# Second slot of a group: the output products first, the value products a slot later, and two PSUM banks that change roles

## The chip, the cores and the metric

One NeuronCore of a Trainium2 chip runs the whole program. The metric is the device time of one execution in microseconds (us), lower is better; a kernel's time is the median of its runs.

## The reference

Attention over pooled keys, then a feed-forward block whose activation is SoLU with a layer norm. Cut to what is computed:

```python
kv_pool = kv.reshape(B, H//4, 4, W//4, 4, C).mean(axis=(2, 4))
k = v = kv_pool.reshape(B, -1, C) @ w_sr          # 768 keys of 128
s = scale * (q @ k.T); a = exp(s - max(s)); a /= a.sum() + 1e-9
x = a @ v                                          # B*N = 49152 tokens of 128
h = x @ w_in                                       # 128 -> 1024
u = h * softmax(h)
ln = (u - mean(u)) / sqrt(var(u) + 1e-6) * g_ln
out = ln @ w_out                                   # 1024 -> 128
```

There are B = 4 batches of N = 12288 tokens. All inputs are float32; the kernel keeps float32-like accuracy by splitting operands in a high and a low 16-bit part and summing three products.

## The kernel before

A tile is 128 tokens, there are 384, and four tiles make a group (96 groups, 24 to a batch). The main loop (lines 892 to 969) runs one slot per tile and is a software pipeline written out by hand: the order of the calls in a slot is the order of the instructions on every engine and on SP's DMA queue, since the program is scheduled by hand. In a slot, work on tiles of very different age stands side by side:

- `scores_pe(slot + 1)`: six products of TensorE (PE) give the scores **s** (L386) of the next tile. `scores_exp`: VectorE (DVE) takes their maximum **nm** (L402), ScalarE (ACT) their exponential (L403) and the high half of the probabilities **phl** (L407). `scores_split`: DVE makes the low half (L415). `scores_turn`: SP turns phl into **pT** by a DMA transpose (L422); below, such a transfer is a *p*.
- `values`: PE multiplies the pT of a whole group with the values in 18 products of 512 columns into one bank **xa** (L453). They are spread over four slots. `values_out` (ACT, **xh**) and `values_split` (DVE, **xl**, L464) read xa out in halves.
- `hidden_pe(slot - 9)`: six products give **h** (L505). DVE takes a minimum **junkd** (L513), ACT an exponential **e** (L529), DVE the product **u** (L543), GpSimd (POOL) the halves **uhl** (L560, L566). `hidden_turn`: SP turns uhl into **uT** by a DMA transpose (L580), below a *u*.
- `final_pe(slot - 13)`: 24 products of 128 columns give a quarter of the bank **o** (L631). `final_half` (L674) scales it to **ob**, two quarters at a time, and `final_store` sends ob out.
- `values_norm` (POOL, **zz**, L479), `values_recip` (DVE, **rz**, L487) and `values_recip_u` (ACT, L492) make a group's scale factors.
- The keys of the next batch are loaded (L216), added on POOL (**ka**, L227), multiplied on PE (**pk**, L235), copied by ACT (L238) and later turned on PE (**pv**, L286) and copied again (L291). `PLAN` (lines 860 to 868) says in which slots of a batch.

Text below names a slot by its number modulo 4: R0, R1, R2, R3. PE's order before is s, xa x4, h, o in R1; xa x1, s, xa x4, h, o in R2 and R3; xa x1, s, xa x3, h, o in R0. In R1 the products of a new group begin in xa and in o.

PSUM has eight banks. Six belong to a ring `ps_r` of three double banks in which s and h take turns: s(slot + 1) takes what h(slot - 11) held and waits for DVE's u; h(slot - 9) takes what s(slot) held and waits for DVE's phl. One bank, `ps_x`, holds xa, and the keys' pk and pv while xa is not in use; the other, `ps_o`, holds o.

SP issues every DMA of the main loop in program order. In R3 it is p, p, u, and then the load of queries **qf**; in R0 u; in R1 p, u and the store; in R2 p, u; and a load of **kv** in many groups.

Of the kernel before, what the change touches and what calls it, by code (L numbers as in the profile page):

```python
# [11 lines left out]
F32 = mybir.dt.float32  # L12
# [6 lines left out]
ALU = mybir.AluOpType  # L19
AX = mybir.AxisListType  # L20

P = 128
# [7 lines left out]
TPB = NTOK // P  # L30
WARM = 14
NT = B * TPB
GT = 4
GPB = TPB // GT
NG = NT // GT
# [9 lines left out]
LAV = 2  # L45
XSP = 5
NORM = 6
LH = 10
LO = 13
FSC = 12  # L50
# [4 lines left out]
ROOM = {NT - 9: 0, NT - 8: 0, NT - 7: 0, NT - 3: 1, NT - 2: 1, NT - 1: 1}  # L55

TAIL = """
U:-1 xa:-1 xh:-1 h:1 o:-4 M:0 xl:-1 J:-1 h:2 hi:-1 E:0 lo:-1 M:1 zz:-1 E:1 o:-3 U:0 h:3
J:0 U:1 zz:0 hi:0 rc:-1 h:4 M:2 ob:-3 rc:0 hi:1 f2:-2 lo:0 rz:-1 E:2 turn:-1 xa:0 turn:0
J:1 lo:1 M:3 st:-3 U:2 o:-2 E:3 J:2 M:4 U:3 E:4 U:4 h:5 xh:0 turn:1 hi:2 f:-2 lo:2 xl:0  # L60
hi:3 J:3 turn:2 M:5 h:6 hi:4 h:7 M:6 E:5 rz:0 lo:3 E:6 o:-1 U:5 M:7 turn:3 o:0 J:4 U:6
f2:-1 o:1 h:8 h:9 o:2 lo:4 E:7 turn:4 U:7 o:3 hi:5 M:8 hi:6 J:5 M:9 ob:-2 lo:5 hi:7 lo:6
# [15 lines left out]
def kernel(  # L78
# [15 lines left out]
    nc = tc.nc  # L94

    dmt = ctx.enter_context(tc.tile_pool(name="dmt", bufs=2))
# [8 lines left out]
    ps_x = ctx.enter_context(tc.tile_pool(name="ps_x", bufs=1, space=bass.MemoryType.PSUM))  # L105
# [34 lines left out]


    state = {}

    def kv_alloc(b):
        for n, w, dt, bufs in (
# [81 lines left out]
        nc.gpsimd.tensor_tensor(ka, x, state["kv", b, pos][:, half, :], op=ALU.add)  # L227

    def kv_psum(b, name):
        pool, tag = (ps_x, "x") if b or name == "pv_0_0" else (ps_o, "o")  # L230
        return pool.tile([P, 512], F32, tag=tag, name=name)

    def kv_k_pe(b, half):
        state["pk", half] = kv_psum(b, f"pk_{b}_{half}")
# [184 lines left out]
    def scores_turn(t):  # L419
        g, j = divmod(t, GT)  # L420
        phl = state.pop(("phl", t))
        nc.sync.dma_start_transpose(  # L422
            state["pT", g][:, j], phl.rearrange("p a h k -> p (a h k)")
        )


    def with_keys(g):


        b, ti = divmod(GT * g + GT - 1 + LAV, TPB)  # L430
        return g > 1 and b + 1 < B and ti in WITH_PE

    def values(g, qtr, part):
        share = {0: [0, 6, 6, 6], 1: [0, 6, 6, 6]}.get(g, [4, 5, 5, 4])
        if with_keys(g):
            share = [3, 5, 5, 5]
        s0 = sum(share[:qtr])
        s1 = s0 + share[qtr]
        if s0 == s1:
            return  # L440
        cut = s0 + (s0 > 0)
        s0, s1 = ((s0, cut), (cut, s1))[part]
        b = g * GT // TPB
        if s0 == 0 and s1:
            state["xa", g] = ps_x.tile([P, 512], F32, tag="x", name=f"xa_{g}")
        if s0 == s1:
            return
        xa, pT = state["xa", g], state["pT", g]
        vh, vl = state["vh", b], state["vl", b]
        seq = [(a, c, v) for c in range(NKC) for (a, v) in ((0, vh), (1, vh), (0, vl))]  # L450
        for n in range(s0, s1):
            a, c, v = seq[n]
            nc.tensor.matmul(  # L453
                xa, v[:, c, :], pT[:, :, a * NKC + c, :], start=n == 0, stop=n == len(seq) - 1
            )
# [157 lines left out]
    def final_pe(t):  # L613
        g, j = divmod(t, GT)
        ts = slice(j * P, (j + 1) * P)
        if j == 0:
            pool, tag = (ps_o, "o") if g != NG - 2 else (ps_x, "x")
            state["po", g] = pool.tile([P, 512], F32, tag=tag, name=f"o_{g}")
        po = state["po", g]
        if t == NT - 1:  # L620
            po = state["po_end"] = ps_r.tile([P, 512], F32, tag="r", name="o_end")
            ts = slice(0, P)
        uT = state.pop(("uT", t))
        seq = []
        for c in range(NFC):
            for n, (a, w) in enumerate(((0, wch), (0, wcl), (1, wch))):
                seq.append((c, a, w, c == 0 and n == 0, c == NFC - 1 and n == 2))
        if t in TURN_PE:
            seq.sort(key=lambda x: x[1])
        for c, a, w, start, stop in seq:  # L630
            nc.tensor.matmul(  # L631
                po[:, ts], uT[:, a * NFC + c, :], w[:, c, :], start=start, stop=stop
            )
# [32 lines left out]
        )  # L666
        state["ob", g, j0] = ob

    def final_half(g, half):
        _, f = state["f", g]  # L670
        if half == 0:
            state["ob", g, 0] = dmt.tile([P, GT, P], F32, tag="ob", name=f"ob_{g}_0")
        js = slice(half * 2, half * 2 + 2)
        nc.vector.scalar_tensor_tensor(  # L674
            state["ob", g, 0][:, js],
            state["po", g][:, half * 256 : half * 256 + 256].rearrange("p (j c) -> p j c", j=2),
            swi,
            f[:, js].unsqueeze(2).to_broadcast([P, 2, P]),
            op0=ALU.mult,
            op1=ALU.mult,  # L680
        )

    def final_store(g, j0=0, j1=GT):
        t0, n = g * GT + j0, j1 - j0
        nc.sync.dma_start(
# [2 lines left out]
        )  # L688

    def final_out(g):  # L690
        final_half(g, 1)
        final_store(g)


# [148 lines left out]
    def w_low():  # L843
# [14 lines left out]


    PLAN = [  # L860
        (69, 0, kv_k_pe, kv_k_out), (73, 1, kv_k_pe, kv_k_out),
        (72, 0, kv_kh), (76, 1, kv_kh),
        (73, 0, kv_kl), (77, 1, kv_kl), (78, 0, kv_kc), (82, 1, kv_kc),
        (75, 0, kv_sq), (77, 1, kv_sq),
        (80, 0, kv_bound), (81, 1, kv_bound), (84, 2, kv_bound),
        (85, 0, kv_v_pe, kv_v_out), (87, 0, kv_v_high), (88, 0, kv_v_low),
        (89, 1, kv_v_pe, kv_v_out), (90, 1, kv_v_high), (91, 1, kv_v_low),
    ]
    WITH_PE = {slot for slot, _, *fs in PLAN if len(fs) > 1}

# [1 line left out]
    def at(t, fn, *args):  # L872
        if 0 <= t < NT:
            fn(t, *args)

    def at_last(t, fn, *args):

        if 0 <= t < NT and t % GT == GT - 1:
            fn(t // GT, *args)

    def at_soon(t, fn):

        at_last(t, fn) if t >= GT else fn(0) if t == GT - 2 else None

    FRONT = (kv_bound,)
    BETWEEN = (kv_kh, kv_sq)
    plan = {}
# [4 lines left out]
    for slot in range(NT):  # L892
        i = slot - LH
        av, qtr = divmod(slot - LAV - GT + 1, GT)
        tb, ti = divmod(slot, TPB)
        if ti == 12 and tb + 1 < B:
            kv_alloc(tb + 1)
        qs = GT if slot < 3 * GT else 3 * GT + QSP
        todo = plan.pop(slot, [])
        for st in todo:  # L900
            if len(st) == 1 and st[0].func in FRONT:
                st[0]()
        if slot == 2:
            kv_bound(0, 0)
        at(slot, scores_exp, [st[0] for st in todo if st[0].func in BETWEEN])
        if slot <= LH:
            at(slot - 1, scores_split)
            at(slot - 1, scores_turn)
        at(i - 1, hidden_u)
        at_last(slot - XSP - 1, values_split)  # L910
        if 0 <= av < NG:
            values(av, qtr, 0)
        at(slot + 1, scores_pe)
        at_soon(slot - NORM, values_norm)
        at_last(slot - FSC, final_scale)
        at(i - 1, hidden_high)
        at(i - 1, hidden_low)
        at_last(slot - FSC, final_root)
        if slot < NT and 0 < qs < slot and (slot - 1 - qs) % GT == 0:
            q_low(slot // GT + 1)  # L920
        if slot < NT - 1:
            at(i - 1, hidden_var)
        at(i, hidden_max)
        at(i, hidden_exp)
        if slot == NT - 1:
            hidden_var(i - 1)
        for f in fill.get(slot, []):
            f()
        pairs = [st for st in todo if len(st) > 1 and st[0].func is not kv_add]
        for st in pairs:  # L930
            st[0]()
        late = 0 <= av < NG and qtr == 0 and with_keys(av)
        if 0 <= av < NG and not late:
            values(av, qtr, 1)
        for st in pairs:
            for f in st[1:]:
                f()
        if slot >= LH:
            at(slot, scores_split)
            if slot == LH:  # L940
                scores_turn(slot)
            elif slot > LH:
                for t in (slot - 1, slot):
                    if t > LH and (t % GT == GT - 1) == (t == slot):
                        scores_turn(t)
        at_soon(slot - NORM, values_recip)
        at_soon(slot - NORM, values_recip_u)
        at(i + 1, hidden_pe)
        at_last(slot - LO, final_half, 0)
        if slot < NT - 1:  # L950
            at(slot - LO, final_pe)
        if late:
            values(av, qtr, 1)
        at(i - 1, hidden_turn)
        at_last(slot - LO - 1, final_out)
        at_last(slot - XSP, values_out)
        for st in todo:
            if st[0].func is kv_add:
                for f in st:
                    f()  # L960
            elif len(st) == 1 and st[0].func not in (*FRONT, *BETWEEN, kv_load):
                st[0]()
        if slot % GT == GT - 1:
            q_load(slot // GT + 3)
        for st in todo:
            if st[0].func is kv_load:
                st[0]()
        if slot < NT and 0 < qs <= slot and (slot - qs) % GT == 0:
            q_split(slot // GT + 1)
# [61 lines left out]
```

## Time and profile before

| | us |
|---|---|
| median of 3 runs | 1850.93 |
| lowest, highest | 1848.46, 1852.03 |
| profiled execution | 1848.9 |
| its span, first to last instruction | 1847.1 |
| busy: PE, DVE, ACT, POOL | 1821.1, 1784.9, 1752.8, 1613.8 |
| DMA moved | 431.8 MB |

The span is what the trace covers; 1.8 us of the profiled execution lie outside it. Every engine but POOL is busy 95% of the span or more, so shares of busy time alone do not say which engine sets the pace. The profile has a row for every instruction, its start and duration, and what ended the idle time before it; from those the stretches are told apart in which PE runs without a pause and those in which it waits.

### The profile page before, as it was taken

To read this page: it belongs to the slowest core of one execution; us is meant where nothing else is said; L and a number is where in the kernel's file an instruction comes from. 1 tells how busy PE (TensorE), PEld (TensorE's weight loads), DVE (VectorE), ACT (ScalarE), POOL (GpSimd) and SP (SyncE) were. 2 spreads that over 40 slices of the span, in tenths; PEclk is the share of its full clock that TensorE was granted. 3 is DMA by queue.
4 is the path that set the end of the run, shared out by engine and by line. 5 is a ranking of instruction groups with operands and counts; after the bars stand their busy time and mean duration, and the time that the engine had idled before them with its cause. 6 is when DMAs were issued, how large, how long until landed. Compare 5 with 4: busy or idle time off the path is not lost.

```text
span 1847.1 us, 43152 instructions
## 1 busy us (share of the span) xinstructions
PE 1821.1 (99%) x15717; PEld 1179.2 (64%) x15718; DVE 1784.9 (97%) x2729; ACT 1752.8 (95%) x3148; POOL 1613.8 (87%) x1392
## 2 busy tenths in 40 slices
PE   8999999999999999999999999999999999999999
PEld 4566666666666666666666666666666666666666
DVE  7999999999999999999999999999999999999998
ACT  6999999999999999999999999999999999999998
POOL 3899889899998999989988899989888888888887
PEclk9999999999999999999999999999999999999999
DMA  8999999999999999999999999999999999999998
GB/s 300 208 238 233 229 245 234 236 240 245 232 234 240 244 238 241 235 233 238 235 233 234 247 241 241 238 236 231 227 217 230 233 228 223 230 227 231 224 223 179
DMA packets 1473253, 431.80 MB, mean 234 GB/s; under 512 B 1400977, under 2 KB 1454353, under 8 KB 1472785
## 3 DMA queue, kind: packets, MB, share of 16 engines
q1 hardware_dynamic: 1472752, 428.98, 114.1%
q8 instruction: 124, 2.03, 0.5%
q14 instruction: 89, 0.72, 0.1%
q10 hardware_dynamic: 288, 0.07, 0.0%
HBM read 52.50 MB, written 25.17 MB: 42 GB/s over the span
## 4 chain that ended last, share of the span: by engine, by line
PE 63%; DVE 13%; ACT 7%; POOL 7%; issue 7%; DMA 3%; DVEq 0%; POOLq 0%; ACTq 0%
PE o L631 19%; PE h L505 18%; PE xa L453 13%; PE s L386 13%; DVE junkd L513 3%; DVE nm L402 3%; POOL uhl L566 3%; DVE phl L415 2%; ACT e L529 2%; DMA pT<-phl 2%; ACT junk L603 2%; POOL uhl L560 2%; ACT phl L407 2%; DVE u L543 1%; DVE ob L674 1%
## 5 line engine op out<-in xcount | busy, mean ns | idle before, releaser
L566 POOL TENSOR_TENSOR uhl<-u,uhl 128x1024 f16<-128x1024 f32 x382 | 815.1, 2134 | 31.7 <-ACT uhl L558 0.2
L631 PEld LDWEIGHTS <-uT 128*128 128x128 f16 x9072 | 537.1, 98 | 91.9 <-DMA uT<-uhl 7.0
L631 PE MATMUL o<-wch,uT 128*128 128x128 f16 x6048 | 568.0, 219 | 1.3 <-DMA uT<-uhl 1.3
L631 PE MATMUL o<-wcl,uT 128*128 128x128 f16 x3024 | 525.9, 219 | 0.0
L560 POOL TENSOR_SCALAR uhl<-u 128x1024 f16<-128x1024 f32 x377 | 393.5, 1044 | 136.2 <-DVE u L543 131.1
L543 DVE SCALAR_TENSOR_TENSOR u<-h,rz,e 128x1024 f32<-128x1024 f32 x384 | 491.2, 1279 | 16.0 <-ACT e L529 3.6
L513 DVE TENSOR_SCALAR_CACHE_REDUCE junkd<-h,rz 128x1024 bf16<-128x1024 f32 x384 | 491.5, 1280 | 1.4 <-PE h L505 1.0
L529 ACT ACTIVATE e<-h,nm,rz 128x1024 f32<-128x1024 f32 x384 | 459.0, 1195 | 1.0 <-DVE junkd L513 1.0
L603 ACT ACTIVATE junk<-u,su 128x1024 bf16<-128x1024 f32 x384 | 437.8, 1140 | 0.2 <-DVE u L543 0.2
L402 DVE TENSOR_REDUCE nm<-s 128x1 f32<-128x768 f32 x384 | 365.7, 952 | 23.3 <-PE s L386 20.8
L453 PE MATMUL xa<-pT,vh 128*128 128x512 f16 x1152 | 373.5, 379 | 6.6 <-DMA pT<-phl 4.0
L403 ACT ACTIVATE s<-s,nm 128x768 f32<-128x768 f32 x384 | 335.9, 875 | 41.9 <-DVE nm L402 37.1
L415 DVE SCALAR_TENSOR_TENSOR phl<-s,phl 128x768 f16<-128x768 f32 x384 | 366.3, 954 | 4.5 <-ACT phl L407 4.3
L407 ACT ACTIVATE phl<-s 128x768 f16<-128x768 f32 x384 | 311.0, 810 | 11.7
L505 PEld LDWEIGHTS <-xh 128*128 128x128 f16 x1536 | 144.8, 97 | 191.7 <-issue 26.7
L386 PE MATMUL s<-kh,qh 128*128 128x384 f32 x768 | 248.0, 404 | 0.1
L505 PE MATMUL h<-w_in_h,xh 128*128 128x512 f16 x768 | 228.2, 379 | 3.5 <-DVE rz L487 2.4
L505 PE MATMUL h<-w_in_h,xl 128*128 128x512 f16 x768 | 228.4, 379 | 0.0
L505 PE MATMUL h<-w_in_l,xh 128*128 128x512 f16 x768 | 228.3, 379 | 0.0
L453 PE MATMUL xa<-pT,vl 128*128 128x512 f16 x576 | 218.3, 379 | 0.0
L386 PE MATMUL s<-kc,ql 128*128 128x384 bf16 x768 | 187.8, 326 | 7.4 <-DVE phl L415 4.4
L386 PE MATMUL s<-kl,qf 128*128 128x384 bf16 x768 | 192.2, 332 | 0.1
(127 smaller groups left out, 1707.2 us busy)
## 6 DMA issues: line engine op xcount, KB each, us to landing
kv<-in_kv_dram SPq DMA_DIRECT2D x64, 384.0 KB, 4.3
qf<-in_q_dram SPq DMA_DIRECT2D x96, 256.0 KB, 3.3
out_dram<-ob SPq DMA_DIRECT2D x95, 256.0 KB, 2.8
pT<-phl SPq DMA_TRANSPOSE x384, 3.8
uT<-uhl SPq DMA_TRANSPOSE x378, 4.4
raw_in<-in_moe_w_in_dram SPq DMA_DIRECT2D x1, 1024.0 KB, 5.4
raw_out<-in_moe_w_out_dram SPq DMA_DIRECT2D x1, 1024.0 KB, 8.6
out_dram<-ob SPq DMA_DIRECT2D x1, 192.0 KB, 2.0
```

Source lines behind the costliest of these rows:

```text
L386: nc.tensor.matmul(s[:, half, :384], lh[:, ts], rh[:, half * 384 : (half + 1) * 384], start=n == (t == 0), stop=n == 2,)
L402: nc.vector.tensor_reduce(nm, s, axis=AX.XY, op=ALU.max, negate=True)
L415: nc.vector.scalar_tensor_tensor(phl[:, 1], state.pop(("s", t)), SC, phl[:, 0], op0=ALU.mult, op1=ALU.subtract)
L453: nc.tensor.matmul(xa, v[:, c, :], pT[:, :, a * NKC + c, :], start=n == 0, stop=n == len(seq) - 1)
L505: nc.tensor.matmul(h[:, hs], lh[:, ts], rh[:, hs], start=n == 0, stop=n == 2)
L513: nc.vector.tensor_scalar(junk, state["h", t], state["rz", g][1][:, j : j + 1], None, op0=ALU.mult, op1=ALU.min, accum_out=nm,)
L529: nc.scalar.activation(e, state["h", t], AF.Exp, bias=nm, scale=state["rz", g][0][:, js], accum_out=state["z2", g][:, js],)
L543: nc.vector.scalar_tensor_tensor(u, state.pop(("h", t)), state["rz", g][2][:, j : j + 1], state.pop(("e", t)), op0=ALU.mult, op1=ALU.mult, ...
L560: nc.gpsimd.tensor_scalar(uhl[:, 0, :], u, 1.0, 1.0, op0=ALU.mult, op1=ALU.mult)
L566: nc.gpsimd.tensor_tensor(uhl[:, 1, :], u, uhl[:, 0, :], op=ALU.subtract)
L603: nc.scalar.activation(junk, u, AF.Square, scale=-float(DFF), bias=su, accum_out=state["v3", g][:, j : j + 1],)
L631: nc.tensor.matmul(po[:, ts], uT[:, a * NFC + c, :], w[:, c, :], start=start, stop=stop)
```

## The change

Six edits, of which the order of each engine follows:

1. In R1, PE runs o before h and has no value products; the first nine of the group stand in R2, five before s and four behind it. R3 and R0 stay.
2. xa and o of successive groups use the two banks in turn (`bank(n)`): xa of group n takes `ps_x` or `ps_o` by the parity of n, o of group n the other. So xa begins in the bank which the o two groups older has just left.
3. ob is one instruction of 512 columns in R1 (`final_mul`, before L659) in place of two of 256 in R0 and R1.
4. zz and rz stand three and two slots earlier: zz in R2 in place of R1, rz and `values_recip_u` in R3 in place of R1.
5. In R3, SP turns u between the two p.
6. The key products pk and pv stand a slot later, in R2, at its head; in those slots all nine value products stand behind s, since pk and pv use the bank ahead of xa.

```diff
 TAIL = """
-U:-1 xa:-1 xh:-1 h:1 o:-4 M:0 xl:-1 J:-1 h:2 hi:-1 E:0 lo:-1 M:1 zz:-1 E:1 o:-3 U:0 h:3
-J:0 U:1 zz:0 hi:0 rc:-1 h:4 M:2 ob:-3 rc:0 hi:1 f2:-2 lo:0 rz:-1 E:2 turn:-1 xa:0 turn:0
+U:-1 xa:-1 xh:-1 h:1 o:-4 M:0 xl:-1 J:-1 h:2 hi:-1 E:0 lo:-1 M:1 E:1 o:-3 U:0 h:3
+J:0 U:1 zz:0 hi:0 h:4 M:2 ob:-3 rc:0 hi:1 f2:-2 lo:0 E:2 turn:-1 xa:0 turn:0
...
+    def bank(n, name):
+        return (ps_x, ps_o)[n % 2].tile([P, 512], F32, tag="xo"[n % 2], name=name)
...
     def kv_psum(b, name):
-        pool, tag = (ps_x, "x") if b or name == "pv_0_0" else (ps_o, "o")
-        return pool.tile([P, 512], F32, tag=tag, name=name)
+        return bank(state["slot"] // GT - 1 if b else name != "pv_0_0", name)
...
-        share = {0: [0, 6, 6, 6], 1: [0, 6, 6, 6]}.get(g, [4, 5, 5, 4])
-        if with_keys(g):
-            share = [3, 5, 5, 5]
+        share = {0: [0, 6, 6, 6], 1: [0, 6, 6, 6]}.get(g, [0, 9, 5, 4])
...
+        if s0 == 0 and g > 1 and not with_keys(g):
+            cut = 5
...
-            state["xa", g] = ps_x.tile([P, 512], F32, tag="x", name=f"xa_{g}")
+            state["xa", g] = bank(g, f"xa_{g}")
...
-            pool, tag = (ps_o, "o") if g != NG - 2 else (ps_x, "x")
-            state["po", g] = pool.tile([P, 512], F32, tag=tag, name=f"o_{g}")
+            state["po", g] = bank(g + 1, f"o_{g}")
...
-        final_half(g, 1)
+        final_mul(g)
         final_store(g)
...
-        (69, 0, kv_k_pe, kv_k_out), (73, 1, kv_k_pe, kv_k_out),
+        (70, 0, kv_k_pe, kv_k_out), (74, 1, kv_k_pe, kv_k_out),
...
-        (85, 0, kv_v_pe, kv_v_out), (87, 0, kv_v_high), (88, 0, kv_v_low),
-        (89, 1, kv_v_pe, kv_v_out), (90, 1, kv_v_high), (91, 1, kv_v_low),
+        (86, 0, kv_v_pe, kv_v_out), (87, 0, kv_v_high), (88, 0, kv_v_low),
+        (90, 1, kv_v_pe, kv_v_out), (91, 1, kv_v_high), (92, 1, kv_v_low),
...
+    def at_z(slot, behind, fn):
+        if slot < 5 * GT:
+            at_soon(slot - NORM, fn)
+        if slot - behind >= 3 * GT:
+            at_last(slot - behind, fn)
...
-        at_soon(slot - NORM, values_recip)
-        at_soon(slot - NORM, values_recip_u)
-        at(i + 1, hidden_pe)
-        at_last(slot - LO, final_half, 0)
+        at_z(slot, ZREC, values_recip)
+        at_z(slot, ZREC, values_recip_u)
+        parts = [partial(at, i + 1, hidden_pe)]
         if slot < NT - 1:
-            at(slot - LO, final_pe)
-        if late:
-            values(av, qtr, 1)
+            parts.append(partial(at, slot - LO, final_pe))
+        for f in parts[::-1] if slot % GT == 1 and slot > 4 * GT + 1 else parts:
+            f()
         at(i - 1, hidden_turn)
+        if slot > LH and slot % GT == GT - 1:
+            scores_turn(slot)
```

**PE's order, from slot 209 (R1) on.** The names carry the tile (s, h, uT) or the group (xa, o, pT). Of each run of products the first stands here. Before:

```order
L386 MATMUL s_210_15110<-kc_2_7681,ql_52_14888 128x384
...
L453 MATMUL xa_51_15131<-pT_51_14766,vh_2_7687 128x512
...
L505 MATMUL h_200_15142<-w_in_h_95,xh_50_15096 128x512
...
L631 MATMUL o_49_15149<-wch_97,uT_196_15025 128x128
...
L386 MATMUL s_211_15190<-kc_2_7681,ql_52_14888 128x384
```

and now:

```order
L391 MATMUL s_210_15068<-kc_2_7666,ql_52_14835 128x384
...
L635 MATMUL o_49_15087<-wch_97,uT_196_14984 128x128
...
L510 MATMUL h_200_15112<-w_in_h_95,xh_50_15054 128x512
...
L458 MATMUL xa_51_15135<-pT_51_14727,vh_2_7672 128x512
...
L391 MATMUL s_211_15141<-kc_2_7666,ql_52_14835 128x384
```

o, which needs the uT of tile 196, stands where xa stood, which needs all four p of group 51; the work between two s is the same in kind and number.

**SP's order in slot 211 (R3).** Before:

```order
L422 DMA_TRANSPOSE pT_52_15059<-phl_210_15184 128x12x128
L422 DMA_TRANSPOSE pT_52_15059<-phl_211_15250 128x12x128
L580 DMA_TRANSPOSE uT_200_15316<-uhl_200_15266 128x16x128
L345 DMA qf_55_15318<-in_q_dram 128x512
```

and now:

```order
L427 DMA_TRANSPOSE pT_52_15019<-phl_210_15130 128x12x128
L585 DMA_TRANSPOSE uT_200_15274<-uhl_200_15221 128x16x128
L427 DMA_TRANSPOSE pT_52_15019<-phl_211_15205 128x12x128
L350 DMA qf_55_15277<-in_q_dram 128x512
```

The u of the tile that opens the next o is one place earlier, the last p of a group one place later.

**DVE's order from slot 209 (R1) to the end of slot 210 (R2).** Before:

```order
L464 SCALAR_TENSOR_TENSOR xl_50_15098<-xa_50_14839,xh_50_15096 128x512
...
L415 SCALAR_TENSOR_TENSOR phl_209_15104<-s_209_15039,phl_209_15104 128x768
L487 RECIPROCAL rz_50_15118<-zz_50_15117 128x8
L674 SCALAR_TENSOR_TENSOR ob_48_0_15068<-o_48_14857,swi_100,f2_48_14973 128x256
L402 TENSOR_REDUCE nm_210_15181<-s_210_15110 128x1
...
L415 SCALAR_TENSOR_TENSOR phl_210_15184<-s_210_15110,phl_210_15184 128x768
```

and now:

```order
L469 SCALAR_TENSOR_TENSOR xl_50_15056<-xa_50_14845,xh_50_15054 128x512
...
L420 SCALAR_TENSOR_TENSOR phl_209_15062<-s_209_14999,phl_209_15062 128x768
L663 SCALAR_TENSOR_TENSOR ob_48_0_15121<-o_48_14796,swi_100,f2_48_14929 128x512
L407 TENSOR_REDUCE nm_210_15127<-s_210_15068 128x1
...
L420 SCALAR_TENSOR_TENSOR phl_210_15130<-s_210_15068,phl_210_15130 128x768
```

rz has left the place between phl and the next nm, and the ob there has 512 columns in place of 256.

## Rows read from the trace of the kernel before

**Rows 1.** The page, busy time, share of the span and count by engine.

```profile
PE 1821.1 (99%) x15717; PEld 1179.2 (64%) x15718; DVE 1784.9 (97%) x2729; ACT 1752.8 (95%) x3148; POOL 1613.8 (87%) x1392
```

**Rows 2.** Windows: stretch, its length, busy us (count) of PE, PEld, DVE, ACT, POOL; clock, DMA share, GB/s.

```profile
200.00:1200.00 1000.00, 990.61 (x8619) 642.02 (x8617) 974.52 (x1491) 956.39 (x1719) 907.45 (x783) 1.00 1.19 238
...
1350.00:1800.00 450.00, 450.00 (x3947) 293.33 (x3945) 444.27 (x682) 435.66 (x777) 378.13 (x316) 1.00 1.13 227
```

**Rows 3.** What PE waited for ahead of xa (us, times), from line L453.

```profile
  DMA pT<-phl: 8.2, 16
```

**Rows 4.** Timeline of SP late in the first stretch: start, us, instruction.

```profile
1194.01 4.04 SPq L422 DMA_TRANSPOSE pT<-phl  x2
1198.15 1.73 SPq L580 DMA_TRANSPOSE uT<-uhl  x1
1199.98 0.53 SPq L345 DMA_DIRECT2D qf<-in_q_dram  x1
1200.61 2.75 SPq L580 DMA_TRANSPOSE uT<-uhl  x1
```

**Rows 5.** The same view in the second stretch.

```profile
1430.45 1.38 SPq L422 DMA_TRANSPOSE pT<-phl  x1
1432.43 1.70 SPq L580 DMA_TRANSPOSE uT<-uhl  x1
```

**Rows 6.** Timeline of PE where xa waited for the transfers of Rows 4.

```profile
1200.42 0.59 PE L453 MATMUL xa<-pT,vh 128*128 128x512 f16 x2 [0.55 <-DMA pT<-phl]
```

**Rows 7.** Issue to landing of p, from line L422.

```profile
DMA to landing us min/median/max: 3.2/3.8/6.4
```

**Rows 8.** Issue to landing of u, from line L580.

```profile
DMA to landing us min/median/max: 3.6/4.4/7.1
```

**Rows 9.** The chain of waits from 800 to 840 us: start, us, run of products.

```profile
804.17 0.65 PE pk L235 x2
...
806.13 1.34 PE o L631 x24
```

**Rows 10.** Timeline of PE in an R1 and an R2 of the second stretch.

```profile
1406.22 0.49 PE L386 MATMUL s<-kc,ql 128*128 128x384 bf16 x2
...
1407.24 0.59 PE L453 MATMUL xa<-pT,vh 128*128 128x512 f16 x2
...
1408.15 0.59 PE L505 MATMUL h<-w_in_h,xh 128*128 128x512 f16 x2
...
1410.78 0.38 PE L453 MATMUL xa<-pT,vh 128*128 128x512 f16 x1
1411.00 0.49 PE L386 MATMUL s<-kc,ql 128*128 128x384 bf16 x2
...
1412.88 0.59 PE L505 MATMUL h<-w_in_h,xh 128*128 128x512 f16 x2
```

**Rows 11.** Timeline of DVE in the same two slots.

```profile
1407.05 0.95 DVE L415 SCALAR_TENSOR_TENSOR phl<-s,phl 128x768 f16<-128x768 f32 x1
1407.92 0.20 DVE L487 RECIPROCAL rz<-zz 128x8 f32<-128x8 f32 x1
1408.03 0.44 DVE L674 SCALAR_TENSOR_TENSOR ob<-o,swi,f 128x256 f32<-128x256 f32 x1
1408.38 0.95 DVE L402 TENSOR_REDUCE nm<-s 128x1 f32<-128x768 f32 x1
...
1410.44 0.09 DVE L543 DVE_READ_ACCUMULATOR u<-h,rz,e 128x1 f32 x1
...
1411.64 0.95 DVE L415 SCALAR_TENSOR_TENSOR phl<-s,phl 128x768 f16<-128x768 f32 x1
```

**Rows 12.** Line L659, ob of 512 columns, in the kernel's tail: ns min/median/max.

```profile
L659 DVE SCALAR_TENSOR_TENSOR ob<-o,swi,f x4: 617/748/749, 1814.9 to 1843.1; 128x512 f32<-128x512 f32 x3, 128x384 f32<-128x384 f32 x1
```

**Rows 13.** The list of waits: h behind pk and pv (us, times, longest).

```profile
PE h L505 <- DVE rz L487: 2.4, 7, 0.7
```

**Rows 14.** The page, traffic of the chip's memory.

```profile
HBM read 52.50 MB, written 25.17 MB: 42 GB/s over the span
```

More of the change, by code (lines that the diff above doesn't have):

```diff
@@ L47 @@
 NORM = 6
+ZSUM = 3
+ZREC = 4
 LH = 10
@@ L427, in with_keys @@
     def with_keys(g):
-        b, ti = divmod(GT * g + GT - 1 + LAV, TPB)
+        b, ti = divmod(GT * g + GT + LAV, TPB)
         return g > 1 and b + 1 < B and ti in WITH_PE
     def values(g, qtr, part):
-        share = {0: [0, 6, 6, 6], 1: [0, 6, 6, 6]}.get(g, [4, 5, 5, 4])
-        if with_keys(g):
-            share = [3, 5, 5, 5]
+        share = {0: [0, 6, 6, 6], 1: [0, 6, 6, 6]}.get(g, [0, 9, 5, 4])
         s0 = sum(share[:qtr])
@@ L667, in final_mul @@
         state["ob", g, j0] = ob
[L669 to L681, printed above, removed]
     def final_store(g, j0=0, j1=GT):
@@ L899 @@
         todo = plan.pop(slot, [])
+        state["slot"] = slot
+        pairs = [st for st in todo if len(st) > 1 and st[0].func is not kv_add]
+        for st in pairs:
+            st[0]()
         for st in todo:
@@ L905 @@
         at(slot, scores_exp, [st[0] for st in todo if st[0].func in BETWEEN])
+        for st in pairs:
+            for f in st[1:]:
+                f()
         if slot <= LH:
@@ L913 @@
         at(slot + 1, scores_pe)
-        at_soon(slot - NORM, values_norm)
+        at_z(slot, ZSUM, values_norm)
         at_last(slot - FSC, final_scale)
@@ L928 @@
             f()
[L929 to L933, printed above, removed]
+        if 0 <= av < NG:
             values(av, qtr, 1)
-        for st in pairs:
-            for f in st[1:]:
-                f()
         if slot >= LH:
@@ L942 @@
             elif slot > LH:
-                for t in (slot - 1, slot):
-                    if t > LH and (t % GT == GT - 1) == (t == slot):
-                        scores_turn(t)
-        at_soon(slot - NORM, values_recip)
-        at_soon(slot - NORM, values_recip_u)
-        at(i + 1, hidden_pe)
-        at_last(slot - LO, final_half, 0)
+                if slot - 1 > LH and slot % GT:
+                    scores_turn(slot - 1)
+        at_z(slot, ZREC, values_recip)
+        at_z(slot, ZREC, values_recip_u)
+        parts = [partial(at, i + 1, hidden_pe)]
         if slot < NT - 1:
-            at(slot - LO, final_pe)
-        if late:
-            values(av, qtr, 1)
+            parts.append(partial(at, slot - LO, final_pe))
+        for f in parts[::-1] if slot % GT == 1 and slot > 4 * GT + 1 else parts:
+            f()
         at(i - 1, hidden_turn)
+        if slot > LH and slot % GT == GT - 1:
+            scores_turn(slot)
         at_last(slot - LO - 1, final_out)
```

## The prediction

> **What bounds the kernel now.** I read the shares of busy time first, and they decide nothing: PE 99%, DVE 97%, ACT 95%, POOL 87% [rows 1]. So I cut the span into windows. From 1350 to 1800 us PE is busy 450.00 of 450 us: nothing makes it wait, and the time there is the sum of its products. From 200 to 1200 us it is busy 990.61 of 1000 us, so 9.4 us are lost [rows 2]. That loss is nearly all that a reordering can give, since the change neither adds nor removes a product.
>
> The waits name the loser: xa, the first value products of a group, waited 8.2 us in 16 places for pT [rows 3]. pT comes through SP's queue, so I went there. Late in the first stretch SP issues without a pause: two p for 4.04 us, the next transfer 0.10 us after their end, the next 0.10 us after that, and so on [rows 4]. In the second stretch there are holes: a p ends at 1431.83 and the next transfer starts at 1432.43, 0.60 us later [rows 5]. The two stretches differ in the key loads, which are over before 1350 us. **So in the first stretch the queue of DMAs is the pace, and PE's waits are how PE falls back to it; in the second it is PE.** The wait at 1200.42 us shows the link: xa starts there after 0.55 us of idle time, released by the p's of rows 4 [rows 4, 6].
>
> **The change, part by part.** All terms are against the profiled execution, 1848.9 us, which is 2.0 under the median of the runs, 1850.93.
>
> *The order of R1 and R2.* Between two s the work stays the same, so PE's own time changes by 0. xa, with its four p, is needed o plus h later: 1410.78 less 1408.15 is 2.63 us for both [rows 10]. That is more than the 0.55 us of the wait in rows 6, so the waits on pT at this place go. But o takes xa's place right behind s, and o needs a u: by 2.2 us earlier than before, four xa and the six h.
>
> *u between two p.* The same edit on SP pays for that need, and the question is whether in full. In rows 4 the two p take 4.04 us; a p of the second stretch takes 1.38 [rows 5], so the second of the two began at 1198.05 less 1.4, about 1196.6, and with the median of 3.8 us from issue to landing it lands at 1200.4, where xa did start [rows 6, 7]. In the new order the u is issued in this place. Its median is 4.4 us [rows 8], so it lands at 1201.0: o would start **0.6 us later than xa did**. The p behind it is issued 1.73 + 0.1 us later [rows 4], at 1198.4, and lands at 1202.2; xa needs it at 1201.0 + 2.63 = 1203.6, so it no longer waits. The wait on pT is thus not removed but handed to u, and is 0.6 us deeper.
>
> How often is that paid? If SP has no holes, its times do not depend on PE. PE then leaves the loaded stretch as late as its last wait on the queue says, and the waits before only divide the way there. So I charge it once: **+0.6 us**. If every one of the 16 waits paid it, it would be 9.6 us (a rival below). At the other end, were u to land like a p, it is 0.
>
> *ob in one piece; rz moved.* In R1 an instruction of 256 columns (0.35 us to the next start, 1408.03 to 1408.38) and rz (0.11 us, 1407.92 to 1408.03) give way to one of 512 [rows 11]. That one has 0.748 us in the tail [rows 12]; as 0.44 us of duration were 0.35 us of pitch, I take 0.66 for it. DVE's chain in R1 grows by 0.66 - 0.46 = 0.20 us; in R0 it loses 0.35, in R3 it gains 0.11. Who notices? In R2, h starts at 1412.88, 0.29 us after phl ends at 1412.59 [rows 10, 11]. In R1 h starts at 1408.15, 0.15 after phl's end at 1408.00, and s and xa ahead of it took 0.05 us longer than those of R2 (1.93 against 1.88): that h is waiting, so 0.15 us is what a wait costs in signalling alone. In R2 the slack would be 0.29 - 0.20 = 0.09, and h waits 0.06. In R1, o (1.34 us [rows 9]) in place of four xa (0.86) gives phl 0.48 us more, so its 0.05 goes. Net **0**. Bounds: 0.05 better to 0.15 worse per group (ob at its full 0.75 us, with no overlap), over some 26 groups of the second stretch -1.3 to +4.
>
> The new xa takes the bank that ob frees. ob would end near 1407.92 + 0.75 = 1408.7 us, xa would begin at 1406.22 + 1.02 + 1.34 + 1.30 = 1409.9 us [rows 9 to 11]: 1.2 us to spare, so 0.
>
> *zz and rz earlier.* Same instructions, on POOL, DVE and ACT, in slots further from their use: 0. zz now stands ahead of the uhl of R2 instead of R1; what it delays there is a u that is not the first of an o.
>
> *Keys.* Twelve slots. Before, h behind pk and pv waited 2.4 us in 7 places [rows 13]. Now pk leads R2 with 0.65 us [rows 9] where five xa took 1.08, so the next s comes 0.43 us earlier: near 1410.5 in the slots of rows 10. It must wait for u, which ends at 1410.53, moved by 0.20, plus 0.15 for the signal: 1410.9, a wait of 0.35 us [rows 10, 11]. Eight of the twelve lie in the loaded stretch and are covered by the queue there; the last four cost 1.4 us in place of their share of the old waits, about 0.7: **+0.7**. Bounds 0 and +3.
>
> Sum: 0.6 + 0 + 0.7 = +1.3, so 1850.2 for the profiled execution and 1852.2 on the scale of the median; I say **1852**.
>
> **The rivals.** *(a) The wait on pT was a matter of order only, and goes: faster.* For it: rows 3 name pT, it gains 2.63 us, and DMA that is late because of what stands ahead of it, not because the queue is full, would be cured. Against: rows 4 have no hole in which SP could catch up. Price: 8.2 us less, keys +0.7: 1843.4; with all 9.4 us gone and the old key waits (2.4) too, 1839. The Trainium skill, Perfetto Trace Analysis, section Identifying the Most-Contended Engine, says to judge DMA by memory utilization and not by its occupancy. By that rule the queue here is far from a limit, at 42 GB/s [rows 14], and (a) would be the forecast; the holes in SP's timeline speak for the occupancy.
>
> *(b) Every wait on u is paid: slower.* o in R1, behind the queue that is late in each loaded group; it decides if SP's lateness is renewed in every group and not carried over. 16 x 0.6 = 9.6, keys 0.7: 1861.
>
> *(c) DVE's longer R1 makes h of R2 wait in every group: slower.* It decides if ob costs over 0.1 us more than I take. 0.15 us over 26 groups is 4, with the other terms 1856; over all 92 it is 14 and 1866, if the queue does not cover it.
>
> **How the numbers follow.** Forecast, no change beyond the queue's shift: 0.46, own range 1848 to 1856. (a): 0.33. (b): 0.13. (c): 0.08. A measurement can tell 0.2%, 3.7 us, from no change. So faster 0.33, same 0.46, slower 0.21. The range runs from 1839, the floor of (a), to 1860, which leaves out the larger part of (b) and the worst of (c), and is for the rest no wider than the two signs make it.
>
> **What would show it.** Right: in 200 to 1200 us PE still loses 8 to 11 us; SP still has no holes there; the waits on pT ahead of xa are near 0 and PE's waits ahead of o on uT have grown to about 8 to 12 us. In 1350 to 1800 us PE is still never idle. ob has about 0.75 us and h of R2 starts 0.15 us behind phl. Wrong: PE's loss in the first window drops below 4 us, and SP's timeline there shows holes or shorter issues (then the queue was not the pace); or PE is idle after 1350 us (then DVE is).

## Result: 0.84% slower, where no change was forecast

| | before | after |
|---|---|---|
| median (lowest to highest), us | 1850.69 (1848.46 to 1852.03), 4 runs | 1866.84 (1864.11 to 1868.55), 4 runs |
| ratio, 95% interval | | 1.0084 [1.0065, 1.0104] |
| profiled execution, its span, us | 1848.9, 1847.1 | 1866.6, 1864.8 |

The time lies outside the range of the forecast, on the side of rival (b). The page of the changed kernel, busy time by engine; it answers to [rows 1] and again decides nothing:

```profile
PE 1826.9 (98%) x15718; PEld 1180.4 (63%) x15718; DVE 1775.0 (95%) x2637; ACT 1745.4 (94%) x3148; POOL 1614.1 (87%) x1392
```

The windows (stretch, length, busy us of PE, PEld, DVE, ACT, POOL; clock, DMA share, GB/s) decide it. First two of the start, then the two stretches of [rows 2]:

```profile
40.00:60.00 20.00, 16.39 (x80) 8.09 (x79) 15.62 (x24) 17.95 (x35) 13.59 (x16) 0.91 0.91 203
60.00:80.00 20.00, 17.18 (x98) 8.85 (x99) 17.69 (x27) 17.66 (x32) 18.27 (x16) 0.91 0.89 194
...
200.00:1200.00 1000.00, 979.49 (x8518) 634.08 (x8516) 956.96 (x1419) 941.15 (x1696) 895.25 (x774) 1.00 1.18 235
...
1350.00:1800.00 450.00, 449.63 (x3927) 292.38 (x3925) 440.93 (x656) 431.69 (x778) 379.49 (x319) 1.00 1.13 228
```

In the second stretch PE is still never idle for long (0.4 of 450 us). In the first it loses 20.5 us where it lost 9.4. **The loss is a matter of the stretch with key loads.** What PE waited for ahead of o (line L635) and ahead of xa (line L458), in us and times; the first answers to a wait of 8.3 us in 18 places before, the second to [rows 3]:

```profile
  DMA uT<-uhl: 47.9, 64
```

```profile
  issue: 3.0, 13
```

Such a row adds up the idle time of PE and of its weight loader, so it overstates what PE loses. (The 8.2 us of [rows 3], which the prediction took for PE's loss ahead of xa, were 4.0 of PE and 4.2 of the loader.) Measured on the products instead, as the time from one product's start to the next beyond its usual step, the gap between s and xa in R1 came to 9.1 us over slots 21 to 377 before, and the gap between s and o in R1 comes to 20.7 now. xa waits for no transfer any more.

One of these waits in full: PE's timeline in an R1, and SP's ahead of it.

```profile
567.11 0.50 PE L391 MATMUL s<-kl,qf 128*128 128x384 bf16 x2
569.68 0.23 PE L635 MATMUL o<-wch,uT 128*128 128x128 f16 x1 [2.06 <-DMA uT<-uhl]
```

```profile
560.73 2.17 SPq L585 DMA_TRANSPOSE uT<-uhl  x1
562.99 1.43 SPq L427 DMA_TRANSPOSE pT<-phl  x1
564.52 2.43 SPq L585 DMA_TRANSPOSE uT<-uhl  x1
567.04 1.91 SPq L427 DMA_TRANSPOSE pT<-phl  x1
569.04 0.53 SPq L350 DMA_DIRECT2D qf<-in_q_dram  x1
```

The u between the two p is issued at 564.52, in a queue without pauses, and o starts 5.2 us later, when it has landed. New, too, are holes in SP's queue in the first stretch, which had none over 0.45 us before (one of 0.67 in e18). The largest stand in the groups with key products, as here, 1.36 us ahead of a u:

```profile
406.71 1.59 SPq L427 DMA_TRANSPOSE pT<-phl  x1
409.66 2.07 SPq L585 DMA_TRANSPOSE uT<-uhl  x1
411.82 1.50 SPq L427 DMA_TRANSPOSE pT<-phl  x1
```

By place, from the starts of the score products in both traces: those of slot 21 (called 20 in the expectations) start 3.2 us later (109.6 against 106.4), slots 21 to 377, the main loop, take 13.4 us more (1683.6 against 1670.2), the end 1.1. In the second pair of profiles, e17 against e18 below, the three parts come to 2.1, 8.7 and 0.9 us: the size of the loss in the main loop differs from execution to execution.

### The profile page after: what moved, and what is told of

It reads as the page before. It is cut to its first block, busy times and chain, and to the rows that moved or that the text cites. A ratio compares the mean times of both kernels' runs of the same rounds, so it can differ in the third digit from the quotient of the medians.

```text
span 1864.8 us, 43068 instructions
## 1 busy us (share of the span) xinstructions
PE 1826.9 (98%) x15718; PEld 1180.4 (63%) x15718; DVE 1775.0 (95%) x2637; ACT 1745.4 (94%) x3148; POOL 1614.1 (87%) x1392
## 4 chain that ended last, share of the span: by engine, by line
PE 63%; DVE 11%; POOL 10%; issue 7%; DMA 7%; ACT 3%; SPq 0%; POOLq 0%; DVEq 0%; ACTq 0%
PE o L635 18%; PE h L510 17%; PE s L391 14%; PE xa L458 14%; DMA uT<-uhl 6%; POOL uhl L571 4%; POOL uhl L565 3%; DVE nm L407 3%; DVE u L548 2%; DVE phl L420 2%; DVE junkd L518 2%; POOL ql L367 1%; DVE xl L469 1%; POOL f L653 1%; DVE ob L663 1%
## 5 line engine op out<-in xcount | busy, mean ns | idle before, releaser
L635 PEld LDWEIGHTS <-uT 128*128 128x128 f16 x9072 | 535.1, 98 | 105.8 <-DMA uT<-uhl 33.8
L635 PE MATMUL o<-wch,uT 128*128 128x128 f16 x6048 | 568.5, 219 | 18.0 <-DMA uT<-uhl 14.1
L635 PE MATMUL o<-wcl,uT 128*128 128x128 f16 x3024 | 526.1, 219 | 0.0
L458 PE MATMUL xa<-pT,vh 128*128 128x512 f16 x1152 | 359.2, 380 | 0.0
L412 ACT ACTIVATE phl<-s 128x768 f16<-128x768 f32 x384 | 311.2, 810 | 11.8
L458 PE MATMUL xa<-pT,vl 128*128 128x512 f16 x576 | 218.6, 379 | 0.0
```

Of the source, the lines that this page charges most:

```text
L458: nc.tensor.matmul(xa, v[:, c, :], pT[:, :, a * NKC + c, :], start=n == 0, stop=n == len(seq) - 1)
L635: nc.tensor.matmul(po[:, ts], uT[:, a * NFC + c, :], w[:, c, :], start=start, stop=stop)
```

## The experiments

Ratios are to the kernel before on the same chip.

### SP's order in R3 and the start

e1 is the changed kernel with p, p, u; e2 with u, p, p; e3 the kernel before with the changed kernel's p, u, p and nothing else of the change:

```diff
 e1, R3 of the changed kernel:
-  scores_turn(slot - 1); hidden_turn(i - 1); scores_turn(slot)
+  scores_turn(slot - 1); scores_turn(slot); hidden_turn(i - 1)
 e2:
+  hidden_turn(i - 1); scores_turn(slot - 1); scores_turn(slot)
 e3, R3 of the kernel before:
-  scores_turn(slot - 1); scores_turn(slot); hidden_turn(i - 1)
+  scores_turn(slot - 1); hidden_turn(i - 1); scores_turn(slot)
```

Expected of e1: 

> The changed kernel with SP's old order in R3 (p, p, u), all else as changed; its time 1866.8. Theory A, the wait for u is paid anew in each loaded group: o in R1 comes as early as now, u is issued one p later (1.4 to 2.0 us), so each of the some 28 waits ahead of o grows by that: 1866.8 + 28 x 1.7 = about 1914, and some waits are added. Theory B, a queue without holes sets the pace and PE is only shifted against it once: +1.7, 1868.5. Theory C, the loss is not in the queue at all (DVE's ob, the banks, the keys): no change, 1867.

Expected of e2: 

> The changed kernel with u ahead of both p in R3 (u, p, p). Theory A: u is issued a p earlier (1.4 to 2.0 us), more than the 0.74 us that a wait ahead of o takes on average, so these waits (20.7 us between s and o in the main loop) go; the last p is issued where it is now, and xa in R2 had no wait for it. What is left is the rest of the loss: 1846 to 1852, no slower than the kernel before. Theory B (shifted once): 1865. Theory C: 1867.

Expected of e3: 

> The kernel before (1850.7) with nothing but SP's order of the change, p, u, p in R3. Theory A: the last p comes behind u, 1.7 us later, and xa stands right behind s: each of the some 22 waits for pT grows by 1.7 us: 1850.7 + 37 = 1888. Theory B: +1.7, 1852. If u was what bound the kernel before, it gets faster.

Measured: e1 1860.52 us (1.0059 [1.0037, 1.0082]), e2 1863.54 (1.0071 [1.0053, 1.0089]), e3 1865.76 (1.0079 [1.0061, 1.0098]). Theory A, as many us more as the u is later at each wait, falls with e1: the u is a whole p later, and the time does not rise at all. Theory B, once, falls with e3: one exchange in SP's order costs 15 us. And e2, which gives o its u earlier, gains nothing that the intervals can tell. PE's windows of e1 and e3, 200 to 1200 us:

```profile
200.00:1200.00 1000.00, 978.45 (x8514) 635.69 (x8513) 955.72 (x1418) 941.01 (x1696) 895.62 (x774) 1.00 1.18 235
```

```profile
200.00:1200.00 1000.00, 976.95 (x8486) 633.54 (x8484) 960.80 (x1469) 942.57 (x1693) 892.91 (x770) 1.00 1.18 235
```

PE loses 21.6 and 23.1 us, as in the changed kernel, but at other products: in e1 nearly all of it at o of R1; in e2 at xa (7.8), at o of R3 (7.6) and of R0 (5.6); in e3 at xa (26.4; these over slots 21 to 377). **The waits go where the order puts them; their sum hardly changes.** Of these four kernels and the one before, only the kernel before, with its own order on PE and on SP, loses clearly less.

e4 puts o ahead of h in R1 from slot 13 on, e15 does that together with e1:

```diff
-for f in parts[::-1] if slot % GT == 1 and slot > 4 * GT + 1 else parts:
+for f in parts[::-1] if slot % GT == 1 and slot > LH else parts:
```

Expected of e4: 

> The changed kernel with o ahead of h in R1 from slot 13 on and not from slot 21 on. In the trace of the changed kernel h waits right behind s for phl in slots 13 and 17, 1.73 and 0.88 us, and the score products of slot 20 start 3.2 us later than before. If these two waits are lost time: 1866.8 - 2.6 = 1864.2. If the start is set by something else (the first u), no change.

Expected of e15: 

> The changed kernel with SP's old order p, p, u in R3 (1860.5 alone) and o ahead of h from slot 13 on (1861.1 alone, against 1866.8). If the two add up: 1855. If the start is one loss that both take away: 1860.

Measured: e4 1861.09 us (1.0058 [1.0040, 1.0075]), e15 1861.43 (1.0059 [1.0046, 1.0072]). The two edits do not add up, and each interval touches that of the changed kernel. In the changed kernel the h of slots 13 and 17 wait right behind s, the longest of such waits here:

```profile
71.34 1.01 PE L510 MATMUL h<-w_in_h,xh 128*128 128x512 f16 x2 [1.57 <-DVE rz L492]
```

In e4 that h stands behind o and waits 0.24 us. But the score products of slot 21 start at 107.0 us in e4 and at 107.1 in e2, which has the changed kernel's start: the edit moves the wait only. In the changed kernel's profile it is 109.6, with a granted clock of 0.91 from 40 to 80 us (the windows above; a mean, since for a part of it TensorE ran at the lower of its two levels, 1.2 GHz in place of 2.4). In e2, e4 and the first profile of the kernel before the clock is 1.00 there. So of the 3.2 us at the start about 0.7 belong to the order, and the other 2.5 came with the clock. That part is not the same each time: e17, the changed kernel again, has 0.91 in both windows too and comes to 108.8 us; e18, the kernel before again, has 0.91 from 40 to 60 us and comes to 106.7.

### The key loads: issues, bytes, bursts, place

e5 (changed) and e6 (before) load the keys in pairs, half as many DMAs of twice the size; e7 (changed) and e8 (before) leave every other load out. In e5 and e6 the buffers change with the loads, to five of twice the size in place of nine:

```diff
 e5, e6:
-t = dmt.tile([P, 2, 384], ...); nc.sync.dma_start(t, kv[b - 1, r, :, two * NK : (two + 1) * NK])
+if two: return
+t = dmt.tile([P, 4, 384], ...); nc.sync.dma_start(t, kv[b - 1, r])
 ...
 e7, e8:
-            yield slot, [partial(kv_load, b, pos)]
+            if pos % 2 == 0:
+                yield slot, [partial(kv_load, b, pos)]
```

Expected of e5: 

> The changed kernel (1866.8) with the key loads in pairs: half as many DMAs on SP's queue, each of twice the size, the same bytes, the same computation. In the traces a key load holds SP for 0.57 us and 0.1 us lies behind it; some 21 fewer are 14 us less for the queue. Theory P, SP's time per issue is the pace of the loaded stretch (in the changed kernel it is busy with the 577 DMAs from 169 to 1201 us for 1022 of 1031.6 us): the time falls by 10 to 14 us, to 1853 to 1857. Theory Q, the bytes are what the transposes contend with: no change, 1867, and each key load takes twice as long to issue. Theory L, o stands too close behind the landing of its u, whatever the queue's load: most of the loss stays, 1863 or more.

Expected of e6: 

> The kernel before (1850.7) with the key loads in pairs. Theory P: SP's queue needs 1014.5 of the 1019.2 us before, PE lost 9.4 us in 200 to 1200; with 14 us less for the queue that loss falls to 1 to 3 us: 1843, and the distance to the changed kernel with pairs shrinks from 16 to 10 or less. Theory Q: no change, 1851. Theory L: xa behind s keeps its waits on pT, 1849 or more.

Expected of e7: 

> The changed kernel with only every other key load of batches 2 to 4 (each tile of keys is added twice, so half of the keys is left out): half the issues and half the bytes. Theory P: as with pairs, 1853 to 1857. Theory Q: only here, not with pairs, the time falls. Theory L: 1863 or more.

Expected of e8: 

> The kernel before with only every other key load of batches 2 to 4 (half of the keys is left out). Theory P: as with pairs, 1843. Theory Q: the time falls here and not with pairs. Theory L: 1849 or more.

Measured: pairs 1870.55 us (1.0112 [1.0094, 1.0130]) and 1858.53 (1.0051 [1.0039, 1.0063]): e6 is slower than the kernel before, e5 not clearly slower than the changed kernel, whose interval it meets. Every other load 1843.41 (0.9968 [0.9956, 0.9980]) and 1838.06 (0.9940 [0.9927, 0.9953]): by the ratios 21 us faster than the changed kernel and 11 faster than the kernel before, and the two stand 5.3 us apart in place of 16. Theory P falls, and with it my reading of a load's price as the 0.57 us in which it holds SP. Theory Q is right on e7 and e8; its "no change" for the pairs fails in e6, and a load of twice the size does not take longer to issue. SP's timeline around a load, before and in e6:

```profile
524.41 0.57 SPq L216 DMA_DIRECT2D kv<-in_kv_dram  x1
525.09 1.40 SPq L422 DMA_TRANSPOSE pT<-phl  x1
526.58 2.87 SPq L580 DMA_TRANSPOSE uT<-uhl  x1
```

```profile
548.76 0.57 SPq L223 DMA_DIRECT2D kv<-in_kv_dram  x1
549.44 1.42 SPq L428 DMA_TRANSPOSE pT<-phl  x1
550.95 5.26 SPq L586 DMA_TRANSPOSE uT<-uhl  x1
```

The load's own issue is the same for twice the bytes; the u two places behind pays. Over the 37 loads between 165 and 1200 us that u takes 3.0 us on SP on average (2.3 for the others), behind a pair 4.9; the p behind a load lands after 5.1 us (about 4.1 for the others), behind a pair after 7.0. So **what a load costs is paid by the transposes behind it, and grows with its bytes**. In e6 PE loses 19.0 us of 200 to 1200, with the order and the slack of the kernel before:

```profile
200.00:1200.00 1000.00, 981.01 (x8530) 634.90 (x8528) 965.07 (x1476) 946.49 (x1701) 897.20 (x774) 1.00 1.19 236
```

PE's windows of e7 and e8, 200 to 1200 us, and what o waited for in e7 (47.9 in 64 places with all loads):

```profile
200.00:1200.00 1000.00, 995.81 (x8676) 647.50 (x8674) 972.11 (x1446) 956.27 (x1729) 912.29 (x789) 1.00 1.18 233
```

```profile
200.00:1200.00 1000.00, 998.03 (x8705) 649.82 (x8703) 981.70 (x1505) 966.47 (x1736) 915.86 (x790) 1.00 1.19 233
```

```profile
  DMA uT<-uhl: 3.8, 8
```

e9 and e10 issue each load of the changed kernel one and two slots earlier (ends of R3 and R2, in place of R0), e11 one slot earlier in the kernel before, e12 issues the loads of the kernel before from ACT:

```diff
 e9, e11 (e10 with 10):
-            slot = max(ADDS[pos] - 8, 8 if b == 1 else -32)
+            slot = max(ADDS[pos] - 9, 8 if b == 1 else -33)
 e12:
-        nc.sync.dma_start(
+        queue = nc.sync if b == 1 and pos in SOON else nc.scalar
+        queue.dma_start(
```

Expected of e9: 

> The changed kernel (1866.8) with each key load issued a slot earlier, at the end of R3 behind qf, in place of R0 behind u. In the traces a p right behind a key load lands after 5.1 us (others 4.0) and the u behind that p holds SP for 3.1 us (others 2.3). Theory S, such a delay costs PE time when it reaches the products with the least slack, o of R1, whose u is issued in R3: with the load in R3's end there are three more slots before the next such u and not two, so less reaches it: 1857 to 1864. Theory T, only the total load of the queue counts: no change, 1867.

Expected of e10: 

> The changed kernel with each key load issued two slots earlier, at the end of R2, just ahead of p, u, p of R3. Theory S: the u that o of R1 waits for lands some 0.9 us later in each group with a load, so PE waits longer: 37 loads by 0.3 to 0.9 us, 1877 to 1900. Theory T: no change, 1867.

Expected of e11: 

> The kernel before (1850.7) with each key load at the end of R3. Its tightest products are xa and o of R1, both fed in R3. Theory S: 1844 to 1849. Theory T: no change, 1851.

Expected of e12: 

> The kernel before with the key loads of the main loop issued from ACT's queue instead of SP's. If the transposes are late because they stand behind the load in SP's queue: PE's loss of 9.4 us shrinks to 2 to 5, 1843 to 1846. If they are late because the load's bytes take the DMA engines from them, whatever the queue: no change, 1851. If ACT pays for the issues (0.57 us each as on SP, ACT is busy 956 of 1000 us there): slower, up to 1860.

Measured: e9 1864.32 us (1.0078 [1.0064, 1.0091]), e10 1871.66 (1.0117 [1.0100, 1.0135]), e11 1857.83 (1.0047 [1.0030, 1.0064]), e12 1877.30 (1.0139 [1.0097, 1.0181]). The signs of theory S are there in the changed kernel, its sizes are not: straight ahead of the critical u a load costs 0.1 us each and not 0.3 to 0.9, and out of its way it gains nothing that can be told. In the kernel before the move costs, against both theories, and its runs spread from 1848.0 to 1864.4 us, the whole way between the two kernels; the profiled one is the fastest, so no trace shows where the slow ones lose. e12 lies beyond all three expectations. The loads no longer stand ahead of anything on SP there, and the next u pays all the same: it holds SP for 4.3 us on average (2.3 for the others). A part of e12's time is the clock's: 0.99 in 200 to 1200 us in the profile, 0.993 to 0.998 over its runs, where the kernel before has 0.999 or 1.000. ACT's issue, then SP's:

```profile
541.85 0.33 ACTq L217 DMA_DIRECT2D kv<-in_kv_dram  x1
```

```profile
541.11 1.66 SPq L581 DMA_TRANSPOSE uT<-uhl  x1
542.86 0.53 SPq L346 DMA_DIRECT2D qf<-in_q_dram  x1
543.49 4.40 SPq L581 DMA_TRANSPOSE uT<-uhl  x1
```

e13 (changed) and e14 (before) issue each load in two halves, in R0 and R1; e16 stores ob in R3 of the changed kernel, behind the last p:

```diff
 e13, e14:
-            yield slot, [partial(kv_load, b, pos)]
+            for half in range(2):
+                yield slot + half, [partial(kv_load, b, pos, half)]
 ...
 e16:
-        final_store(g)
...
         at_last(slot - LO - 1, final_out)
+        at_last(slot - LO - 3, final_store)
```

Expected of e13: 

> The changed kernel with each key load of the main loop in two DMAs of half the size, one in R0 and one in R1: same bytes, 37 more issues between 165 and 1200 us. Theory S (a burst against the slack of the product that waits): each transposes' delay is halved, more of them stay below the slack of o in R1 (3.3 us in the second stretch): 1855 to 1863. Theory Q (sum of the bytes): no change, 1867. If the number of issues counts after all (37 x 0.67 = 25 us on SP): 1870 to 1890.

Expected of e14: 

> The kernel before with the same halves. Theory S: 1842 to 1848, a version that beats both. Theory Q: no change, 1850. If issues count: 1855 to 1870.

Expected of e16: 

> The changed kernel with the store of ob two slots later, in R3 behind the last p, in place of R1; ob itself stays. Theory S: the store (0.58 us on SP, 0.26 MB) no longer stands ahead of the u that o of R1 waits for, but has the three slots behind it to be worked off: PE waits less ahead of o in R1, 1858 to 1865. Theory Q: same bytes, 1867.

Measured: e13 1864.48 us (1.0075 [1.0062, 1.0089]), e14 1853.01 (1.0019 [1.0009, 1.0029]), e16 1862.83 (1.0070 [1.0058, 1.0083]). Halving the bursts gains nothing: the interval of e13 meets that of the changed kernel, and e14 is 0.2% slower than the kernel before. e16 lies in the range of theory S, but its interval too meets that of the changed kernel. So theory S is not borne out. Theory Q, the sum of the bytes, fits these three best, but it is not the whole: e6 and e11 move the same bytes as the kernel before and are slower. In e16 the gap at o of R1 falls from 20.7 to 11.8 us and 7.8 come up at o of R3: once more nearly the same sum.

### Both kernels again

Expected of e17: 

> The changed kernel, unedited, profiled a second time. If longer issues on SP are a property of its order: SP again spends some 968 us in the issues of the 577 DMAs (960.7 in the kernel before) and 8.4 us in holes. If not, the sum of both stays near 976.6 and the split moves by more than 5 us.

Expected of e18: 

> The kernel before, unedited, profiled a second time. If its queue is always at work in the loaded stretch: again under 5 us of holes, 958 to 964 us in issues, and PE loses 8 to 11 us in 200 to 1200 us. If the first profile was a lucky one: holes of 5 us or more.

Measured: 1863.16 and 1851.48 us, one execution each. Their windows, changed and before:

```profile
200.00:1200.00 1000.00, 981.96 (x8530) 636.53 (x8529) 958.09 (x1423) 942.29 (x1700) 898.21 (x775) 1.00 1.19 235
```

```profile
200.00:1200.00 1000.00, 989.13 (x8598) 640.88 (x8596) 972.67 (x1488) 955.08 (x1715) 907.02 (x781) 1.00 1.19 237
```

SP's account over the 577 DMAs from p of slot 32 to p of slot 248, summed from the rows of its timeline, from 165 to some 1200 us. Between any two issues lie about 0.1 us, some 55 us in all; what the pauses have beyond that are holes:

| | all, us | in issues | pauses |
|---|---|---|---|
| before, and again (e18) | 1019.2, 1021.5 | 960.7, 962.6 | 58.5, 58.9 |
| changed, and again (e17) | 1031.6, 1030.1 | 968.2, 964.9 | 63.4, 65.2 |
| changed, p p u (e1) | 1032.6 | 959.9 | 72.7 |
| changed, u p p (e2) | 1031.2 | 969.3 | 61.9 |
| before, p u p (e3) | 1034.1 | 961.1 | 73.0 |

The kernel before has the fewest pauses in this table and keeps them the second time. The changed kernel has 5 to 6 us more of them, again the second time, and 2 to 8 us more in issues; of the issues, a part that moves by 3 us between two executions is chance. So holes are 4.9 of the 12.4 us that the queue takes longer in the first pair and 6.3 of 8.6 in the second. The split depends on the order: in e1 and e3 the whole loss of the queue is pauses, in e2 most of it is longer issues. And e6 loses its 19.0 us with pauses of 57.8, as few as in the kernel before: holes are not needed for a loss.

## Why the prediction was wrong

Of the signs that the prediction named, three came: xa no longer waits for pT, PE is hardly idle after 1350 us, and ob has 0.74 us. Three did not: PE loses 20.5 us and not 8 to 11, SP's queue has holes, and o in R1 waits 20.7 us and not 8 to 12.

**What bounds the kernel: right.** The queue in the first stretch, PE in the second. e7 and e8 show it: with fewer bytes in the queue the waits go, in both kernels. Their profiles then lie 6.2 us apart, 1.8 at the start, 3.3 in the main loop, about what the keys below cost, and 1.1 at the end; so the longer ob and the exchange of banks cost nothing that shows.

**ob, rz, zz at 0: right.** ob takes what the tail's did [rows 12]:

```profile
L663 DVE SCALAR_TENSOR_TENSOR ob<-o,swi,f x96: 618/742/748, 92.0 to 1860.6; 128x512 f32<-128x512 f32 x95, 128x384 f32<-128x384 f32 x1
```

h of R2, in the second stretch, timelines of DVE and of PE:

```profile
1428.79 0.95 DVE L420 SCALAR_TENSOR_TENSOR phl<-s,phl 128x768 f16<-128x768 f32 x1
```

```profile
1429.58 0.38 PE L458 MATMUL xa<-pT,vl 128*128 128x512 f16 x1
1429.80 0.60 PE L510 MATMUL h<-w_in_h,xh 128*128 128x512 f16 x2
```

phl ends at 1429.74 and h starts 0.06 later, where 0.09 of the old 0.29 were forecast to be left, one usual step (0.22) behind the last xa: the forecast wait of 0.06 did not come. A group of the second stretch takes 0.02 us less than before. Rival (c) is out.

**Keys at +0.7: mis-sized.** In e7 and e8, where the queue hides nothing, the six key groups of a batch take 1.4 us longer than before in each of the first two batches, and those of the third 0.7: 3.5 us in all, over the upper bound of 3. In the first profiles of the two kernels, with all loads, the same groups take 3.2 us longer. The lists of waits, changed and before, show the mechanism that was named, s waiting for u:

```profile
PE s L391 <- DVE u L548: 3.6, 9, 0.7
```

```profile
PE s L386 <- DVE u L543: 1.3, 3, 0.7
```

e7 has the same 3.6 us in 9 places. The step that failed here is "eight of the twelve lie in the loaded stretch and are covered by the queue there": they are paid with and without the queue's load.

**The wait handed from pT to u: 0.6 us deeper, as forecast.** In the second stretch, from the landing of the last transfer to the product that needs it, medians over 24 groups: xa of R1 had 3.9 us to spare before (its tightest product), o of R1 has 3.3 now (3.8 and 3.2 in e18 and e17).

**"If SP has no holes, its times do not depend on PE. So I charge it once": this step failed.** Take keys (3.5) and the second stretch's small gain (-1.3, 0.02 us over some 65 quiet groups) from the 13.4 us of the main loop, and about 11 us are left for those 0.6; from the 8.7 us of the second pair, 6.5. That SP has no holes was true of the kernel before, but not of the changed one, whose holes stand ahead of a u. And the rest does not follow: each u that SP turns comes from an h, and that h stands behind the waiting o, as it stood behind the waiting xa before, so a wait of PE can come back to SP as a late u. How the loss comes about is not shown. Of what SP's queue takes longer, holes are 5 to 6 us and the rest is longer issues; and e3 shows only that the exchange of u and p on SP, priced here at 0.6, is enough for a loss of this size: 15 us in the kernel before.

Nor was it 16 times 0.6, as rival (b) has it, though its 1861 lay nearest and its 9.6 us lie between 6.5 and 11: e1 makes the slack 1.7 us smaller still (1.6 us) and costs nothing more. So the price of (b) came near by luck. The experiments say this, for loads as they are: with the kernel before's slack of 3.9 us PE loses 9 to 11 us in 200 to 1200; with 3.3, 2.5 (e2), 1.8 (e3 and e15) or 1.6 (e1) it loses 16 (e15) to 23, wherever the slack is taken; with half of the loads' bytes it loses 2 to 4 at either slack. The slack does not decide alone: e6, with loads in pairs, has 4.0 us of it and loses 19.0.

What I make of it, argued and not shown: a queue that may fall 4 us behind keeps enough finished tiles waiting in front of it to work on through the groups with key products, where POOL delivers uhl late and the holes of the changed kernel stand. Where a product catches it at 3 us, PE waits sooner, SP comes to those groups with less in hand, and runs dry. The spread of e11, 1848 to 1864 us for one kernel, would fit a kernel that sits on the edge between the two. Why every changed order ends at 0.6 to 0.8%, and where the 2 to 8 us of longer issues come from, stays open.

**The start and the end, +3.2 and +1.1, were not priced at all.** The order there costs about 0.7 and 1; the 2.5 us that came with the lower clock are no term that the rows before could show.

**Rival (a)** is out: the waits on pT went as it said, and came back at u. The rule that the prediction named in favour of (a) was read too narrowly there. The Trainium skill's page Perfetto Trace Analysis, section Identifying the Most-Contended Engine, has DMA judged by HBM utilization instead of occupancy, and goes on in the same sentence that one then finds which DMA resource actually binds. In its section Engine Utilization that utilization is all that the DMAs move, which is 238 GB/s here [rows 2], and not the 42 GB/s of [rows 14]. The changed kernel's page of the profile shows 42 GB/s again, and e7 and e8 show that the queue is a limit all the same; so 42 GB/s is no sign of a free queue, and the trace does not speak against the Trainium skill's rule.

No kernel that does the whole work beat the one before; e14 came nearest, 0.2% behind.

## What to carry to other kernels

When a queue's work nearly fills a stretch, its lateness may be a store that the consumers' slack makes possible (argued above, not shown): before moving a product, compare the slack from landing to first use of the tightest product in a stretch without waits, old and new, and treat a loss of some tenths as a possible loss of all that the slack held back, neither once nor times the number of waits. A term "covered by" another wait needs its own test, with that wait taken away: the key terms were paid in full. And price a DMA by what the transfers behind it do, not by its own issue.

## What was not expected of the hardware

- A key load holds SP for 0.57 us whether it has 0.39 or 0.79 MB; the DMA transpose two places behind holds SP for 3.0 and 4.9 us on average (2.3 without a load). Issued from ACT, where it takes 0.33 us, the load still makes the next u on SP take 4.3 on average (e12).
- The granted clock was 0.91 from 40 to 80 us in both profiles of the changed kernel, and 1.00 there in e2 and e4. It is not bound to the kernel: the kernel before has 1.00 in its first profile and 0.91 from 40 to 60 us in e18. The fastest of the four runs of the changed kernel (1864.11 us) has a mean clock of 1.000, the other three 0.998. What brings it about was not found.
- Moving 37 loads by one slot (e11) widened one kernel's runs from 1847 to 1855 us to 1848 to 1864.
